# A gated MLP with a long convolution, forward and backward: regrouping the convolution's 64x32 passes on TensorE

## The chip, the cores and the metric

The kernel runs on one core of a Trainium2 chip. The metric is device time in microseconds, the median of several runs. The core's engines are called PE (TensorE, matrix products), DVE (VectorE), ACT (ScalarE), POOL (GpSimd) and SP (SyncE, which here only issues transfers). Each takes its own instructions in order, and they wait for each other by semaphores.

## The reference

It computes the sum of an input, a long-convolution branch (A) and a gated MLP (B), and the gradients of all weights and inputs from a given output gradient. Cut to what matters:

```python
def A(q, k, v, shift_k, ssm_k, ssm_D):          # S = 2048, D = 1024
    kv = shift4(k, shift_k) * v                  # four taps along time
    y = irfft(rfft(pad(kv)) * rfft(pad(ssm_k)))[:S]   # per channel, length 2 S
    return q * (y + kv * ssm_D)
def B(x, W_gate, W_up, W_down):                  # F = 3584
    gate = x @ W_gate
    return ((gate * (gate > 0)) * (x @ W_up)) @ W_down
xn = layernorm(A_q)
out = A_q + A(xn, k, v, shift_k, ssm_k, ssm_D) + B(xn, W_gate, W_up, W_down)
grads = vjp(out)(grad_out)                       # of all nine inputs but B_x
```

## The kernel before

**Two streams on one PE.** `LnMlp` yields the MLP's work step by step, eight 128x128 by 512 matmuls at a time, each step counted as some 1730 ns. `ABranch.steps` (line 587) yields the convolution as a list of slots. The loop at lines 1791 to 1802 counts nanoseconds and calls the next slot whenever the MLP's steps have paid for the last one: 1900 ns a slot while the MLP's forward part runs, and in the weight-gradient parts (`DENSE`, line 585) 1900 for a slot with products and 1250 for one without. So convolution products always stand between two MLP steps, and the order in each engine is written out by hand.

**The convolution.** The channels are done in eight groups of 128. Each length-4096 transform is factored into two small steps. In a group three spectra are needed: H (the filter), G (the incoming gradient times xn) and K (kv). Three products follow: GKV = H times conj(G), which gives the gradient of kv (`gkv`); K times conj(G), which gives the filter's gradient (`gh`); and K times H, which gives the output (`yt`). `cmul` (line 453) does half a product in five DVE steps; `turn` (446) prepares operands.

**Passes.** A slot may hold products. `fwd1`, `fwd1_filter`, `inv_a` and `inv_a_pair` use 32x64 tiles of PE (a "crossed" slot mixes an inverse step of this group with a forward step of the next). `f2`, `f2_pair` and `inv_b` use 64x32 tiles:

- `f2_pair(j, m)` (429) is the last forward step of G and K at once: two rounds of eight products of 256 columns.
- `f2(F, half, j)` (413) is the same for H alone: four rounds of eight products of 128 columns.
- `inv_b(st, key, half)` (512) is the last inverse step, two units, each one round of eight products of 512 columns.

Each such unit takes two of the eight PSUM banks (`banks`, 71); every bank is copied out by ACT (`act`, 85). A slot takes at most `cap` units: three, or two while the MLP's block of four simultaneous sums (`four`, line 1401) runs; what is over goes into a pass of its own (`parts`, 549). `tensor` (562) orders the rounds of a pass and puts the copies behind them.

**The arena.** One tile of nine parts of 8 KB per partition holds everything (line 132). Between the two small steps the data is turned by DVE transposes (`flip`, 338, two per call) into `flp`, which before is parts 0 and 1. G and K lie interleaved in parts 2 and 3, H in 4, `Cg`, `Ch`, `Cy` in 5 and 6, `Bg` and GKV in 7, `Bk` in 8. Part 0 is used for G before `f2_pair`, then for `gkv`, `yt` and `gh` before `inv_b`; part 1 for H before `f2` and for K before `f2_pair`.

**Loads and stores.** `fetch` (649) puts loads of the next groups into a list, from which one per slot is issued on SP, three slots later at the earliest, and not while `hold` is set (the last rows of an MLP block, or `cap` 2). `need` (272) issues what is still listed. `store` (105) issues on SP three slots later. `halo` (536) copies three rows between partitions.

**One group's passes before**, in order: three pair passes (3, 3 and 2 units), three 32x64 passes, `gkv`, `inv[1]`, crossed, crossed, `inv[2]`, two `f2` units, crossed, crossed, one `f2` unit with `yt`, one `f2` unit with `gh`. The `f2` units are the next group's H.

Of the kernel before, what the change touches and what calls it, by code (L numbers as in the profile page):

```python
# [17 lines left out]
P = 128  # L18
# [30 lines left out]
class ABranch:  # L49
# [27 lines left out]
    def evict(self, parts, view, out):  # L77
        for i, p in enumerate(parts):
            self.act(out(slice(i, i + 1)), p.rearrange(view))
# [49 lines left out]
    def open_arena(self):  # L129
        for _ in range(2):  # L130
            self.pools.pop().release()
        arena = self.pool("a_are", 1, side="right").tile([P, 9, NB1 * P], BF16, name="arena")
        self.flp = arena[:, 0:2, :].rearrange("p e (k c) -> p e k c", c=P)
        self.GK = arena[:, 2:4, :].rearrange("p s x -> p (s x)").rearrange("p (g b k i c) -> p g b k i c", b=2, k=2,
                                                                           i=2, c=P)
        self.G, self.K = self.GK[:, :, :, 0], self.GK[:, :, :, 1]
        spectrum = lambda i: arena[:, i, :].rearrange("p (g b i c) -> p g b i c", b=2, i=2, c=P)
        rows = lambda i: arena[:, i, :].rearrange("p (b cp u r i) -> p b cp u r i", cp=32, u=2, r=16, i=2)
        half = lambda i: arena[:, i, :].rearrange("p (bc q m i) -> p bc q m i", q=4, m=8, i=2)
        self.Bh = arena[:, 6, :].rearrange("p (b x cp n i) -> p b x cp n i", x=2, cp=16, n=NB1, i=2)  # L140
        self.Bg, self.Bk, self.H, self.GKV = rows(7), rows(8), spectrum(4), spectrum(7)
        self.Cg, self.Ch, self.Cy = half(5), half(5), half(6)
        self.Cs = arena[:, 5:7, :].rearrange("p s x -> p (s x)").rearrange("p (bc q m i) -> p bc q m i", q=4, m=8, i=2)

    def close(self):
# [283 lines left out]
    def f2_pair(self, j, m):  # L429

        def go():
            ps, at = self.banks("e b k i c", b=2, k=2, i=2)

            def part(ri):
                for q in range(4):
                    for e in range(2):
                        rows, l = slice(64 * e, 64 * e + 64), 8 * q + 2 * j + m
                        self.mm(at(e)[32 * q:32 * q + 32, :, :, ri, :], self.FW[rows, l, ri, :],
                                self.flp[rows, :, l, :].rearrange("p k (b c) -> p b k c", b=2))
            return [(256, lambda ri=ri: part(ri)) for ri in range(2)], lambda: self.evict(  # L440
                ps, "p e b k i c -> p (e b k i) c",
                lambda s: self.GK[:, 2 * j + s.start:2 * j + s.stop, :, :, :, 64 * m:64 * m + 64].rearrange(
                    "p e b k i c -> p (e b k i) c"))
        return go
# [117 lines left out]
    def tensor(self, p):  # L562

        if not isinstance(p, list):
            return self.run(p)
        units = [f() for f in p]
        first = [u for u in units if u[0][0][0] == 128][0:1]
        for rounds, _ in first if len({u[0][0][0] for u in units}) > 1 else []:
            rounds.pop(0)[1]()
        for rounds, _ in sorted(units, key=lambda u: -u[0][0][0]):  # L570
            for _, part in rounds:
                part()
        for _, evict in units:
            evict()

# [78 lines left out]
    def first(self, st):  # L654
        f1h, nx = self.fwd1_filter(st)[1], self.ahead(st, 1)
        yield f1h[0], lambda: self.gate_grad(st)
        yield None, None
        yield f1h[1], None
        self.load_k(st)
        f1g = self.fwd1(self.Bg, st["gt"])[1]  # L660
        yield None, lambda: self.add_D(st)
        flH = self.flip_H()
        yield f1g[0], flH
        yield None, flH
        yield f1g[1], None
        self.fetch(nx, self.load_g)
        f2H = [(1, self.f2(self.H, 1, j)) for j in range(4)]
        yield None, None
        flG = self.flip_B(self.Bg, 0)
        yield f2H[0:2], flG  # L670
        yield None, flG
        self.begin(st)
        tk = st["tk"]
        yield None, tk
        yield f2H[2:4], tk
        self.fetch(nx, self.load_xn)
        for _ in range(5):
            yield None, tk
        yield None, lambda: self.start_kvt(st)
        f1k = self.fwd1(self.Bk, st["kvt"])[1]  # L680
        yield None, None
        yield f1k[0], None
        yield None, None
        yield f1k[1], None
        self.fetch(nx, self.load_filter)
        yield None, None
        flK = self.flip_B(self.Bk, 1)
        yield None, flK
        yield None, flK
        yield None, None  # L690

    def slots(self, st, gi):
        G, K, H, GKV = self.G, self.K, self.H, self.GKV
        if gi == 0:
            yield from self.first(st)
        nx, n2 = self.ahead(st, 1), self.ahead(st, 2)
        last = nx is None
        f2 = [(1, self.f2_pair(j, m)) for j in range(4) for m in range(2)]
# [10 lines left out]
        yield None, None  # L709
        yield None, lambda: self.turn(G, 0, -1, slice(0, 4))  # L710
        q = self.cmul(H, G, True, GKV, 0)
        yield f2[6:8], q
        yield None, q
        yield None, q
        yield None, q
# [3 lines left out]
        q = self.cmul(H, G, True, GKV, 1)  # L719
# [13 lines left out]
        q = self.cmul(K, G, True, G, 0)  # L733
# [11 lines left out]
        yield None, q  # L745
        yield None, q
        q = self.cmul(H, K, False, K, 0)
        yield self.inv_b(st, "gkv", 0), q
        yield None, q
        yield None, q  # L750
        gkv = st["gkv"]
        gks = st["gks"] = self.ttile("gks")
        yield None, lambda: self.tt(gks[:, 0:16, :], gkv[:, 0:16, :], st["vt"][:], ALU.mult)
        self.fetch(nx, self.load_v)
        gv = self.ttile("gv")
        yield None, lambda: self.tt(gv[:, 0:16, :], gkv[:, 0:16, :], st["ksh"][:], ALU.mult)
        yield None, q
        self.store(self.gks_d[gi], gks[:, 0:16, :].rearrange("p r c -> p (r c)"))
        yield None, q
        self.store_time(self.out_gv, st["cg"], gv)  # L760
        yield [], lambda: self.halo(st)
        ia, inv = self.inv_a_pair()
        q = self.cmul(K, G, True, G, 1)
        yield None, q
        yield None, q
        yield inv[1], q
        yield None, q
        yield None, q
        q = self.cmul(H, K, False, K, 1)
        cross, gk = [inv[0], None], None  # L770
        if not last:
# [2 lines left out]
            self.fetch(n2, self.load_xn)  # L774
            cross = self.crossed(ia, self.fwd1(self.Bg, nx["gt"])[0], 0)
        yield None, q
        yield None, q
        yield cross[0], q
        yield None, q
        yield None, q  # L780
        f1g, cross = cross[1], [inv[3], None]
        f2H = []
        if last:
            yield None, None
            yield inv[2], None
        else:
            f2H = [(1, self.f2(H, 1, j)) for j in range(4)]
            self.need(self.load_k, nx)
            self.need(self.load_taps, nx)
            self.begin(nx)  # L790
            tk = nx["tk"]
            yield f1g, tk
            self.fetch(n2, self.load_g)
            yield None, tk
            yield None, tk
            yield inv[2], tk
            yield None, tk
            yield None, tk
            yield f2H[0:2], tk
            self.need(self.load_v, nx)  # L800
            yield None, lambda: self.start_kvt(nx)
            cross = self.crossed(ia, self.fwd1(self.Bk, nx["kvt"])[0], 3)
            yield None, None
# [11 lines left out]
        yield None, fly  # L815
        yield None, tg
        yield None, tg
        yield f2H[2:3] + self.inv_b(st, "yt", 0), None
        self.store_time(self.y_d, st["cg"], st["yt"])
        flh = self.flip_C(self.Ch, 0)  # L820
        yield None, flh
# [1 line left out]
        yield None, tg  # L823
        yield None, tg
        self.store_time(self.out_gk, st["cg"], gk)
        yield f2H[3:4] + self.inv_b(st, "gh", 0), None
        if last:
            yield None, None
            yield None, lambda: self.store_gh(st)
            return  # L830
        flG = self.flip_B(self.Bg, 0)
        yield None, flG
        yield None, self.both(lambda: self.store_gh(st), flG)
        flK = self.flip_B(self.Bk, 1)
        yield None, flK
        yield None, flK
        yield None, None
        yield None, None

# [3 lines left out]
class LnMlp:  # L843
# [271 lines left out]
    PACE = (2100, 1350)  # L1115

    def hidden(self, first, goT, load, ln, tables, Wg, Wu, Wd, g, xn_d, h_d, ug_d):


        nc, HS, N = self.nc, self.ST // 2, 2 * self.FB  # L1120
        w, sets, spare = first, (0, 1, 2), 3
        self.g_nat, self.hs = [None] * self.ST, [None] * (self.ST // 2)
        xT, gT = [], goT
# [713 lines left out]
```

## Time and profile before

| | |
|---|---|
| median of 3 runs | 1859.3 us (1858.87 to 1859.62) |
| profiled execution, its own time | 1858.79 us |
| its span | 1857.0 us |
| PE busy | 1850.1 us, 13061 matmuls |
| DVE busy | 1114.1 us |
| ACT busy | 645.7 us |
| SP's DMA queue q1 | 320.31 MB, 71.6% of 16 engines |
| clock granted to PE | 1.0 |
| convolution's first and last product (L83) | 125.0 and 1226.4 us |

The span is what the profile covers; the run's own time is 1.8 us longer. A line of the timeline has the start and length in microseconds, the engine, the kernel's line, the operation, what it writes and reads, the tile (rows*columns), the shape and how many instructions are merged; in brackets idle time before it and what ended it. A line of the waits has who waited, for whom, the microseconds in all, how often, and the longest.

### The profile page before, as it was taken

What the parts mean: (1) busy time and instruction counts of PE and PEld (TensorE: products, weight loads), DVE (VectorE), ACT (ScalarE), POOL (GpSimd) and SP (SyncE); (2) the same over time, 40 slices, a digit from 0 to 9 for tenths busy, and PEclk for the clock granted to TensorE, in tenths of its full rate; (3) what the DMA queues carried; (4) which work ended last, traced back from release to release, by engine and by line L of the source; (5) the groups of instructions that cost most, each with busy time, mean ns of one, the idle gap of its engine ahead of it and who ended that gap; (6) DMA issues with size and microseconds to landing.
All of it is one profiled execution on the core that took longest, in us unless ns stands there. A gap on an engine that the chain in (4) does not pass through costs nothing.

```text
span 1857.0 us, 32063 instructions
## 1 busy us (share of the span) xinstructions
PE 1850.1 (100%) x13061; PEld 845.7 (46%) x13061; DVE 1114.1 (60%) x1635; ACT 645.7 (35%) x1215; POOL 19.4 (1%) x51
## 2 busy tenths in 40 slices
PE   9999999999999999999999999999999999999999
PEld 4444444444444444444444444444444544444444
DVE  6656797797789767685694767621222222566652
ACT  5644444435444445545545454420000000111100
POOL 1000000000000000000000000000000000000000
PEclk9999999999999999999999999999999999999999
DMA  9897689967768766559566454379999857799973
GB/s 264 246 218 185 152 205 207 224 170 183 184 153 216 231 156 165 147 156 233 147 152 163 126 135 145 119 200 275 257 250 220 199 142 167 176 209 207 200 163 74
DMA packets 748132, 344.65 MB, mean 186 GB/s; under 512 B 576088, under 2 KB 715344, under 8 KB 747984
## 3 DMA queue, kind: packets, MB, share of 16 engines
q1 hardware_dynamic: 736848, 320.31, 71.6%
q10 hardware_dynamic: 9504, 17.04, 3.2%
q0 software_dynamic: 1632, 5.24, 0.8%
q8 instruction: 102, 1.67, 0.4%
q14 instruction: 46, 0.38, 0.1%
HBM read 143.79 MB, written 103.83 MB: 133 GB/s over the span
## 4 chain that ended last, share of the span: by engine, by line
PE 98%; SPq 1%; DMA 1%; DVE 0%; ACT 0%; issue 0%; ACTq 0%
PE ps_x L1689 21%; PE ps_w L1393 20%; PE ps_h L1058 10%; PE ps_o L1557 10%; PE ps_u L1058 10%; PE ps_g L1058 10%; PE ps_d L1393 9%; PE ps_c L83 4%; PE ps_d L1409 2%; PE ps_w L1409 1%; SPq L1076 1%; DMA goT<-in_grad_out_dram 0%; PE ps_r L1591 0%; DMA wg<-in_B_W_gate_dram 0%; DVE arena L344 0%
## 5 line engine op out<-in xcount | busy, mean ns | idle before, releaser
L1393 PE MATMUL ps_w<-ugs,xn_nat 128*128 128x512 bf16 x1728 | 381.3, 379 | 0.0
L87 ACT CAST arena<-ps_c 128x512 bf16<-128x512 f32 x576 | 294.0, 613 | 109.2 <-PE ps_c L83 109.0
L1058 PEld LDWEIGHTS <-xnT 128*128 128x128 bf16 x1792 | 172.0, 98 | 209.7 <-issue 5.7
L344 DVE STREAM_TRANSPOSE arena<-arena 128x1024 f32<-128x1024 f32 x96 | 179.5, 1931 | 133.1 <-ACT arena L87 117.0
L1393 PEld LDWEIGHTS <-xn_nat 128*128 128x128 bf16 x1728 | 165.2, 98 | 201.5 <-issue 7.3
L1058 PE MATMUL ps_u<-wu,xnT 128*128 128x512 bf16 x896 | 206.1, 379 | 0.1
L1058 PE MATMUL ps_g<-wg,xnT 128*128 128x512 bf16 x896 | 205.0, 379 | 0.6 <-DVE xnT L1102 0.3
L1058 PE MATMUL ps_h<-wdT,goT 128*128 128x512 bf16 x896 | 204.9, 379 | 0.6 <-DMA goT<-in_grad_out_dram 0.6
L1689 PE MATMUL ps_x<-wgT,ggT 128*128 128x512 bf16 x896 | 198.6, 379 | 0.0
L1689 PE MATMUL ps_x<-wuT,guT 128*128 128x512 bf16 x896 | 198.6, 379 | 0.0
L1707 ACT ACTIVATE w<-xn,m 128x512 f32<-128x512 bf16 x32 | 24.3, 807 | 480.2 <-DVE m L1700 366.8
L1557 PE MATMUL ps_o<-wd,hT 128*128 128x512 bf16 (+1 forms) x896 | 187.6, 372 | 0.0
L1393 PE MATMUL ps_d<-g_nat,hs 128*128 128x512 bf16 x768 | 170.1, 379 | 0.0
L1689 PEld LDWEIGHTS <-guT 128*128 128x128 bf16 x896 | 87.7, 98 | 105.7
L1689 PEld LDWEIGHTS <-ggT 128*128 128x128 bf16 x896 | 87.7, 98 | 105.5
L1058 PEld LDWEIGHTS <-goT 128*128 128x128 bf16 x896 | 85.7, 98 | 105.1 <-issue 2.9
L1557 PEld LDWEIGHTS <-hT 128*128 128x128 bf16 x896 | 87.7, 98 | 99.9
L1301 ACT CAST gh<-ps_h 128x512 bf16<-128x512 f32 x112 | 66.4, 594 | 184.4 <-PE ps_h L1058 175.0
L1396 ACT CAST wi<-ps_w 128x512 bf16<-128x512 f32 x108 | 64.6, 598 | 181.4 <-PE ps_w L1393 150.8
L1173 DVE SCALAR_TENSOR_TENSOR ru<-ru,ps_u 128x512 bf16<-128x512 bf16 x112 | 76.5, 683 | 71.9 <-PE ps_u L1058 49.3
L1549 DVE TENSOR_TENSOR ya<-ya,xe 128x1024 bf16<-128x1024 bf16 x16 | 11.1, 692 | 176.2 <-DMA xe<-xn_d 176.2
L91 DVE TENSOR_TENSOR t<-arena 128x2048 bf16<-128x2048 bf16 x96 | 113.9, 1219 | 0.4
(145 smaller groups left out, 1391.5 us busy)
## 6 DMA issues: line engine op xcount, KB each, us to landing
ugs<-ug_d SPq DMA_DIRECT2D x112, 256.0 KB
ug_d<-ru SPq DMA_DIRECT2D x110, 256.0 KB
wg<-in_B_W_gate_dram SPq DMA_DIRECT2D x56, 256.0 KB
wu<-in_B_W_up_dram SPq DMA_DIRECT2D x56, 256.0 KB
hs<-h_d SPq DMA_DIRECT2D x56, 256.0 KB
out_dram<-wi SPq DMA_DIRECT2D x56, 256.0 KB
h_d<-ht SPq DMA_DIRECT2D x108, 128.0 KB
gt<-in_grad_out_dram SPq DMA_DIRECT2D x32, 256.0 KB
```

What stands on the lines that cost most here:

```text
L83: self.pri.pin(self.nc.tensor.matmul(out, lhsT=lhsT, rhs=rhs, start=start, stop=stop))
L87: self.pri.pin(self.nc.scalar.copy(out=out, in_=in_))
L91: self.pri.pin(self.nc.vector.tensor_tensor(out=out, in0=in0, in1=in1, op=op))
L344: self.pri.pin(self.nc.vector.transpose(out=df[:, c0:c0 + 32, :], in_=sf[:, c0:c0 + 32, :]))
L1058: self.pri.pin(self.nc.tensor.matmul(ps[:], lhsT=xT[:, kt * P:(kt + 1) * P], rhs=w(kt), start=(kt == 0), stop=(kt == self.DT - 1)), always ...
L1173: return self.pri.pin(nc.vector.scalar_tensor_tensor(out=ru[s][:, 1, :], in0=ru[s][:, 0, :], scalar=0.0, in1=ps[:], op0=ALU.is_gt, op1=ALU ...
L1301: self.pri.pin(nc.scalar.copy(out=gh[:], in_=ps[:]))
L1393: self.pri.pin(self.nc.tensor.matmul(ps[:], lhsT=lhsT(st), rhs=rhs(st), start=(st == 0), stop=(st == self.ST - 1)))
L1396: self.pri.pin(self.nc.scalar.copy(out=out, in_=ps[:]))
L1409: self.pri.pin(self.nc.tensor.matmul(ps[i][:], lhsT=lhsT(i, st), rhs=rhs(i, st), start=(st == 0), stop=(st == self.ST - 1)))
L1557: nc.tensor.matmul(ps, lhsT=hT[:, kt, :], rhs=self.wd[:, kt, oc], start=(kt == 0), stop=(kt == self.FT - 1))
L1689: nc.tensor.matmul(ps, lhsT=T[:, kt, :], rhs=W[:, kt, oc], start=(i == 0), stop=(i == n - 1))
```

## The change

- `flp` becomes a view of all nine parts. G is turned into part 8 instead of part 0, after K has been turned out of part 8; `f2_pair` reads parts 1 and 8. G and K change places in their interleaved storage, and `Cy` and `Ch` change parts.
- Part 0 then stays free for `gh`, whose second half goes into the next group's third pair pass, with its stores. The first half shares a pass with the last two `f2` units.
- `gkv` comes six slots later, shares a pass with the first `f2` unit, and what hangs on it (gks, gv, their stores, the halo, the next `vt` load) moves with it; the K times H product moves ahead.
- The slot that held two `f2` units alone has no products any more. The crossed passes of G come one slot earlier.
- `tensor` orders a pass as one short round, the 512-column rounds, the other short rounds; with eight short rounds five come first.

The diff, cut:

```diff
-        self.flp = arena[:, 0:2, :].rearrange("p e (k c) -> p e k c", c=P)
+        self.flp = arena[:, 0:9, :].rearrange("p e (k c) -> p e k c", c=P)
...
-        self.G, self.K = self.GK[:, :, :, 0], self.GK[:, :, :, 1]
+        self.K, self.G = self.GK[:, :, :, 0], self.GK[:, :, :, 1]
...
-        self.Cg, self.Ch, self.Cy = half(5), half(5), half(6)
+        self.Cg, self.Cy, self.Ch = half(5), half(5), half(6)
...
-                                self.flp[rows, :, l, :].rearrange("p k (b c) -> p b k c", b=2))
+                                self.flp[rows, 1:9:7, l, :].rearrange("p k (b c) -> p b k c", b=2))
...
-        first = [u for u in units if u[0][0][0] == 128][0:1]
-        for rounds, _ in first if len({u[0][0][0] for u in units}) > 1 else []:
-            rounds.pop(0)[1]()
-        for rounds, _ in sorted(units, key=lambda u: -u[0][0][0]):
-            for _, part in rounds:
-                part()
+        short = [part for rounds, _ in units for n, part in rounds if n < 512]
+        at = 5 if len(short) == 8 else 1
+        for part in short[:at] + [part for rounds, _ in units for n, part in rounds if n == 512] + short[at:]:
+            part()
...
-        yield f2[6:8], q
+        if gi:
+            pv = self.sts[gi - 1]
+            yield f2[6:8] + self.inv_b(pv, "gh", 0)[1:], q
+            self.store_gh(pv)
+        else:
+            yield f2[6:8], q
...
         q = self.cmul(H, K, False, K, 0)
-        yield self.inv_b(st, "gkv", 0), q
+        for _ in range(5):
+            yield None, q
+        f2H = [] if last else [(1, self.f2(H, 1, j)) for j in range(4)]
+        ia, inv = self.inv_a_pair()
+        q = self.cmul(K, G, True, G, 1)
+        yield None, q
+        yield f2H[0:1] + self.inv_b(st, "gkv", 0), q
         yield None, q
         yield None, q
+        yield inv[1], q
         gkv = st["gkv"]
         gks = st["gks"] = self.ttile("gks")
         yield None, lambda: self.tt(gks[:, 0:16, :], gkv[:, 0:16, :], st["vt"][:], ALU.mult)
         self.fetch(nx, self.load_v)
+        self.store(self.gks_d[gi], gks[:, 0:16, :].rearrange("p r c -> p (r c)"))
         gv = self.ttile("gv")
         yield None, lambda: self.tt(gv[:, 0:16, :], gkv[:, 0:16, :], st["ksh"][:], ALU.mult)
-        yield None, q
-        self.store(self.gks_d[gi], gks[:, 0:16, :].rearrange("p r c -> p (r c)"))
-        yield None, q
         self.store_time(self.out_gv, st["cg"], gv)
-        yield [], lambda: self.halo(st)
...
-        yield None, q
+        yield [], lambda: self.halo(st)
         yield cross[0], q
         yield None, q
         yield None, q
-        f1g, cross = cross[1], [inv[3], None]
+        yield cross[1], q
+        self.fetch(n2, self.load_g)
+        cross = [inv[3], None]
...
-            yield f1g, tk
-            self.fetch(n2, self.load_g)
+            yield None, tk
...
-            yield f2H[0:2], tk
+            yield None, tk
...
-        yield f2H[2:3] + self.inv_b(st, "yt", 0), None
+        yield f2H[1:2] + self.inv_b(st, "yt", 0), None
...
-        yield f2H[3:4] + self.inv_b(st, "gh", 0), None
+        gh = self.inv_b(st, "gh", 0)
         if last:
+            yield gh, None
...
-        flG = self.flip_B(self.Bg, 0)
-        yield None, flG
-        yield None, self.both(lambda: self.store_gh(st), flG)
-        flK = self.flip_B(self.Bk, 1)
+        yield f2H[2:4] + gh[0:1], None
+        flK, flG = self.flip_B(self.Bk, 1), self.flip_B(self.Bg, 8)
         yield None, flK
         yield None, flK
+        yield None, flG
+        yield None, flG
```

The first group's own opening is changed in the same way: G is turned after K, into part 8.

## The prediction

> **What bounds the kernel now.** I read the page's busy shares, the chain that ended last and the table of waits first: they say whether time can be won anywhere but on TensorE.
>
> ```profile
> PE 1850.1 (100%) x13061; PEld 845.7 (46%) x13061; DVE 1114.1 (60%) x1635; ACT 645.7 (35%) x1215; POOL 19.4 (1%) x51
> PE 98%; SPq 1%; DMA 1%; DVE 0%; ACT 0%; issue 0%; ACTq 0%
> PE ps_warm L1113 <- POOL warm L1110: 1.5, 1, 1.5
> PE ps_c L83 <- ACT arena L87: 0.6, 1, 0.6
> ```
>
> PE is busy all the time, 98% of the chain is PE, and PE's longest waits are 1.5 and 0.6 us. So a change of the convolution's order is worth what it changes in PE's own stream, plus any wait that it adds. VectorE (60%) and ScalarE (35%) only have to be early enough.
>
> The second view is PE's timeline around single passes. A pass is one uninterrupted run of convolution products (L83) between matmuls of the MLP.
>
> ```profile
> 732.65 1.89 PE L1393 MATMUL ps_d<-g_nat,hs 128*128 128x512 bf16 x8
> 734.47 0.78 PE L83 MATMUL ps_c<-arena,FW 64*32 64x128 bf16 x64
> 735.18 3.63 PE L1393 MATMUL ps_d<-g_nat,hs 128*128 128x512 bf16 x16
> ...
> 750.78 3.19 PE L1393 MATMUL ps_d<-g_nat,hs 128*128 128x512 bf16 x14
> 753.90 0.25 PE L83 MATMUL ps_c<-arena,FW 64*32 64x128 bf16 x8
> 754.68 3.63 PE L1393 MATMUL ps_d<-g_nat,hs 128*128 128x512 bf16 x16
> ...
> 777.27 0.85 PE L83 MATMUL ps_c<-arena,FW 64*32 64x256 bf16 x48
> 778.05 5.35 PE L1393 MATMUL ps_d<-g_nat,hs 128*128 128x512 bf16 x24
> 783.34 0.63 PE L83 MATMUL ps_c<-arena,FW 64*32 64x256 bf16 x32
> 783.90 2.33 PE L1393 MATMUL ps_d<-g_nat,hs 128*128 128x512 bf16 x10
> ...
> 813.64 2.11 PE L1393 MATMUL ps_d<-g_nat,hs 128*128 128x512 bf16 x9
> 815.68 0.63 PE L83 MATMUL ps_c<-arena,RB 64*32 64x512 bf16 x16
> 816.24 2.12 PE L1393 MATMUL ps_d<-g_nat,hs 128*128 128x512 bf16 x9
> ```
>
> The reader is to take starts, not durations, because matmuls overlap. One MLP matmul takes 0.216 us from start to start (elsewhere 16 of them from 379.89 to 383.35). What a pass inserts is the start of the next MLP matmul minus the place where it would have stood. Two pair units (32 products of 256 columns): 783.90 - (778.05 + 24 x 0.216) = 0.67. Three pair units (48): 778.05 - 777.18 = 0.87, where 777.18 is 776.75 plus two steps. An inverse of two units (16 products of 512): 816.24 - 815.58 = 0.66. Two single forward units (64 products of 128): 735.18 - 734.38 = 0.80. One single forward unit with a whole inverse: 754.68 - 753.80 = 0.88. With the trace's finer digits these are 0.656, 0.874, 0.651, 0.802 and 0.874.
>
> Eight products of these tiles run side by side. From 0.656 to 0.874 two more eights of 256 columns were added, 0.11 each, so four cost 0.44 and **about 0.22 us of each pass is independent of what streams through it**. The 0.651 of the inverse gives the same (two eights of 512 at 0.21).
>
> **The change, part by part.** (1) *Passes.* The products are all kept; only their grouping changes. Per group of channels before: three pair passes (0.874, 0.874, 0.656), gkv alone 0.651, two forward units alone 0.802, forward unit + yt 0.874, forward unit + gh 0.874. After: pair, pair, pair + half of the earlier group's gh, forward + gkv, forward + yt, two forwards + half of gh. The first five have 0.874 each by streaming (0.22 + 0.64). The sixth has eight eights of 128 columns and one of 512: 0.22 + 0.43 + 0.21 = 0.87 plus an unknown e.
>
> Group 0 has no earlier gh and group 7 no forward units, so seven groups change 0.651 + 0.802 + 0.874 + 0.874 = 3.20 into 3 x 0.874 + e = 2.62 + e, and seven times the third pair pass grows by 0.218. The sum is 7 x (-0.58 + 0.22 + e), with the fine digits -2.53 + 7e, and 126 passes instead of 133.
>
> (2) *The unknown e.* No pass of before mixes 64 small products with eight long ones. The nearest rows bound it: the yt pass streams its 48 products with nothing on top (0 above), the pass of 64 small products costs 0.802 where streaming alone would give 0.65 (0.15 above). So e is 0 to 0.15. I take 0.03, near the yt row, since there too a long eight stands ahead of three short ones and gives the issuing time to catch up; only the first five shorts are exposed. The Trainium skill, "TensorE: Matmul & The Clock Gate", section "Architectural detail: the array is 16× 32×32, not 1× 128×128", gives PE a queue of 64 instructions, which 72 products with their weight loads overrun; by that alone e would be near 0.15 and the gain 0.7 us smaller. The yt pass has 96 instructions, overruns it too and pays nothing, so the row decides.
>
> (3) *Splits.* While the MLP's four-at-once blocks (L1401) hold four PSUM banks, a pass may have two units. Adding up the yields of both streams (which puts every pass of before where the trace has it) one of the merged passes falls there, group 2's last: 0.802 + 0.436 instead of 0.874 + e. Before, the same place cost 0.659 + 0.436 instead of 0.874. That is +0.14, and e counts six times. The pair of forward units at 858.38 stood in such a block and cost 0.08 more than its like; it is gone. So far: -2.53 + 0.14 - 0.08 + 6 x 0.03 = -2.29.
>
> (4) *Crossed passes one slot earlier.* In group 4 both crossed passes stand in such a block, and each needs six banks while the block holds up to four.
>
> ```profile
> 839.25 0.30 PE L83 MATMUL ps_c<-arena,IA 32*64 32x256 bf16 x4
> 840.35 0.89 PE L83 MATMUL ps_c<-gt,R 32*64 32x512 bf16 x4 [0.57 <-ACT arena L87]
> 841.17 1.04 PE L1409 MATMUL ps_d<-g_nat,hs 128*128 128x512 bf16 x4
> ```
>
> This first one inserted 2.01 where its like inserts 0.66: 1.35 us for a bank. It stays where it is. The second (846.67) cost nothing; it moves eight matmuls earlier, when one more bank still waits for a copy of some 0.6 us. Bounds 0 and 1.35; I take 0.4.
>
> (5) *Moved VectorE work.* gks, gv, the input's product and both flips change order, 96 transposes and all multiplications stay. In the dense part VectorE has finished the last input of the next pass well ahead: the last flip before a pair pass ends some 3 us ahead, and after the change three of those distances shrink by eight matmuls (1.7 us) to about 1.2 us. Cost 0; with that cover gone, up to 1 us each. (6) *SP and POOL.* gh's stores go some eleven slots later and gks/gv's stores stand ahead of the halo loads, same number; the next vt load is asked for seven slots later. POOL's memset stays in its place. Cost 0, except in the third rival. (7) *The strided read* of parts 1 and 8 in one operand: same columns, another distance; no row shows one, and 0 to the smallest difference between passes (0.02) bounds it, so 0.
>
> Sum: -2.29 + 0.4 = -1.9 us of the profiled execution's 1858.79 (span 1857.0 and 1.8 around it), 1856.9; that execution lies 0.5 under the median, so **1857.4**.
>
> **The rivals.** *ScalarE's copies set the pace.* Fuller passes need six banks at once.
>
> ```profile
> 338.94 3.04 ACT L87 CAST arena<-ps_c 128x512 bf16<-128x512 f32 x6
> 344.64 0.58 ACT L1301 CAST gh<-ps_h 128x512 bf16<-128x512 f32 x1 [2.66 <-DMA h_d<-ht]
> ```
>
> Six copies take 3.04 us; the closest passes are 16 matmuls and one pass apart, 4.3 us, which leaves room for two other copies. But ScalarE takes its work in order: here one copy waited 2.66 us for a store, and the pass at 344.41 inserted 1.46 instead of 0.87. New is that the copy of the first forward unit overwrites H while VectorE's product may still read it. In group 4 that product's fourth step ends about 17.9 us after the pass at 802.80 (its steps taken from 805.63 on), the copy is due at 19.1; 88 matmuls apart instead of 80, the others have 2.8. If VectorE is over 1.2 to 2.8 us later there, ScalarE stands, and each of seven groups pays one such stall, 0.59 to 1.35, say 1.0: 1857.4 + 7 = **1864.4, slower**. The Trainium skill, "TensorEngine Tiling (Array Packing)", section "PSUM Bottleneck", says that tiling quickens TensorE but not the emptying of PSUM, which can become the limit; by it this rival is the likelier one. Against it stand the pairs of six-unit passes of before at the same distance (772.93 and 777.27), without a wait. 5%.
>
> *Issue, not the switch, is the price.* If small products cost 9 ns each (0.58 / 64) wherever they stand, e is 0.15 and the crossed pass pays 0.8: 1859.3 - 2.47 + 0.9 + 0.8 = **1858.5**. 14%.
>
> *A late load.* In group 4 the load of vt for group 5 now becomes due inside a four-at-once block, is held back, and is forced out one slot before its use. A vt load takes 5.3 us from first issue (820.58) to its last small packets (about 826), the product 1.22. Issued behind the eight ugs loads (857.9) it would hold up the next crossed pass by 2 to 3 us: **1859.9**; ahead of them (851.8), as program order has it, nothing. 8%.
>
> *Stalls go as well*: gh's stores leave the crowded place at 344, and the 0.59 and most of 1.35 vanish: **1855.7**. 7%. *It doesn't do what it says*: most merged passes are split by the bank limit and the 0.22 us stay: **1859.3**. 2%.
>
> **How the numbers follow.** The forecast holds 64%: 1857.4. Range 1855.8 to 1860.5: from a little above "stalls go" over both bounds of e and of the crossed pass to the late load. A measurement of this kernel tells about 0.2% (3.7 us) from no change. Faster by more (under 1855.6): the lower half of "stalls go", 4%. Slower by more (over 1863.0): the first rival and a few stalls of other origin, 6%. Within: 90%.
>
> **What would show it.** Right: 126 passes; seven of 0.87 each for pair + gh, forward + gkv; the sixth at 0.87 to 0.92; no new row in PE's waits but some tenths at the second crossed pass near 843. Wrong: the sixth at 1.0 (e), PE rows waiting for "ACT arena" in several groups, or PE waiting for "DVE kp" in group 4.

## The result and the profile after

The changed kernel takes 1866.02 us (median of 6 runs, 1863.39 to 1868.04); the kernel before took 1859.13 (6 runs, 1858.81 to 1859.62) in the same comparison. The ratio is 1.0037 with a 95% interval of [1.0024, 1.005]: slower by 0.37%, where 1857.4 was forecast and 1860.5 was the upper end. The profiled execution took 1868.04 us, its span 1866.3 against 1857.0 before, so 9.3 us have to be found.

The busy line of the page after, some of PE's waits, and PE's and ACT's timelines where the longest wait stands:

```profile
PE 1837.0 (98%) x12845; PEld 848.0 (45%) x13061; DVE 1115.0 (60%) x1635; ACT 645.7 (35%) x1215; POOL 19.4 (1%) x51
```
```profile
PE ps_g L1058 <- ACT gh L1301: 5.6, 1, 5.6
PE ps_w L1393 <- issue: 3.0, 19, 0.2
...
PE ps_c L83 <- DVE kp L91: 0.9, 1, 0.9
PE ps_h L1058 <- DVE ru L1173: 0.7, 1, 0.7
PE ps_c L83 <- DVE arena L344: 0.7, 1, 0.7
```
```profile
340.80 0.85 PE L83 MATMUL ps_c<-arena,FW 64*32 64x256 bf16 x48
341.58 1.90 PE L1058 MATMUL ps_g<-wg,xnT 128*128 128x512 bf16 x7
349.13 3.57 PE L1058 MATMUL ps_g<-wg,xnT 128*128 128x512 bf16 x8 [5.65 <-ACT gh L1301]
```
```profile
339.18 0.58 ACT L1301 CAST gh<-ps_h 128x512 bf16<-128x512 f32 x1 [4.58 <-PE ps_h L1058]
348.49 0.58 ACT L1301 CAST gh<-ps_h 128x512 bf16<-128x512 f32 x1 [8.73 <-DMA h_d<-ht]
348.97 3.04 ACT L87 CAST arena<-ps_c 128x512 bf16<-128x512 f32 x6
```

DVE and ACT do the same work as before, to 0.9 us and to the digit. PE's busy time is no measure here: 216 of 13061 matmul records are missing, and the "issue" row (19 waits of at most 0.2 us) is holes in the record, not time. The weight loads are complete, so all inserted times below go by their starts, as the forecast's went by matmul starts. By this measure a pass of three units inserts 0.883 in the trace of before as well.

The other rows are new. The first is the news: group 1's first pair pass (340.80) has six full banks, and its copies stand on ACT behind the copy of an MLP bank (`gh` of line 1301, not the filter's gradient of the same name) that waits 8.73 us for a store of `ht`, the MLP's hidden block, to land. `ht` and this `gh` take turns in the same five buffers (`e1_tile`), so the copy has nowhere to write until the store has read its buffer. Until 348.49 no bank is emptied, and the MLP runs out of banks after one more sum.

Over what the passes and the MLP would take by their own classes, this execution loses: **8.64 us near 349**, 1.35 at the first crossed pass near 848 (as before), 1.15 at a crossed pass near 871 (waits for `kp`, which waits for vt), 0.80 near 248 (`ru`, the MLP's pair tile, into which DVE empties a bank), 0.78 near 181 (`arena`, a transpose), 0.33 near 323 (`wu`, a load that SP brings late), 0.29 near 329 (`ru` again), 0.51 at the second crossed pass near 854, 0.41 near 642 (a bank that waits for the copies of a six-bank pass), 0.10 near 388. The sixth passes lose 0.68 together. Before had its own: 1.35 near 839, 0.57 near 344, 0.39 near 484. The sum: -2.47 (passes) + 0.68 + 0.51 + 0.78 + 0.80 + 8.64 + 1.15 + 0.62 + 0.41 + 0.10 - 0.57 - 0.39 = +10.3; the first 38 us, which the change doesn't touch, were 1.0 shorter in this execution. That gives 9.3.

### The profile page after: what moved, and what is told of

The parts are those of the page before. It is cut to its first block, busy times and chain, and to the rows that moved or that the text cites. A ratio compares the mean times of both kernels' runs of the same rounds, so it can differ in the third digit from the quotient of the medians.

```text
span 1866.3 us, 31860 instructions
## 1 busy us (share of the span) xinstructions
PE 1837.0 (98%) x12845; PEld 848.0 (45%) x13061; DVE 1115.0 (60%) x1635; ACT 645.7 (35%) x1215; POOL 19.4 (1%) x51
## 4 chain that ended last, share of the span: by engine, by line
PE 94%; DVE 2%; DMA 1%; issue 1%; ACT 0%; SPq 0%; POOL 0%; DVEq 0%; ACTq 0%; POOLq 0%
PE ps_x L1689 21%; PE ps_w L1393 20%; PE ps_o L1557 10%; PE ps_u L1058 10%; PE ps_g L1058 10%; PE ps_h L1058 9%; PE ps_d L1393 9%; PE ps_c L83 4%; PE ps_d L1409 1%; DVE arena L344 1%; DMA vt<-in_A_v_dram 0%; DVE ru L1173 0%; DMA wu<-in_B_W_up_dram 0%; PE ps_r L1591 0%; DMA h_d<-ht 0%
## 5 line engine op out<-in xcount | busy, mean ns | idle before, releaser
L1393 PE MATMUL ps_w<-ugs,xn_nat 128*128 128x512 bf16 x1676 | 374.9, 379 | 4.8 <-issue 3.0
```

The source lines that it names most:

```text
L1393: self.pri.pin(self.nc.tensor.matmul(ps[:], lhsT=lhsT(st), rhs=rhs(st), start=(st == 0), stop=(st == self.ST - 1)))
```

## The experiments

The theory: **the copies of one pair pass stand behind a copy that waits for a late store**. It has two halves, the place of the pass and the lateness of SP. The rival: the loss is the price of fuller passes (the first rival of the forecast), and stands in many places. Each comparison has its own runs of the kernel before on the same chip: 1858.60 us for the first four kernels, 1858.79 for the next four, then 1858.32, 1858.63 and 1858.48.

### Place and stores: four kernels

**shift_after** is the changed kernel with one empty slot less at the end of group 0, **shift_before** the kernel before with one more.

```diff
-        yield None, None
+        if gi:
+            yield None, None
```

> The changed kernel with one empty slot less at the end of group 0, so that group 1's first pair pass stands after 1432 MLP matmuls, as before the change, and not after 1440. Theory 'place': the long wait near 341 us is there because this pass came to stand behind the ScalarE copy that waits for a store; back at its old place the loss there falls from 8.6 to about 0.6 us and the kernel takes 1858 to 1860 us. Rival 'fuller passes': the pass holds six banks wherever it stands and the merged passes are what costs; the time stays at 1863 to 1868 us.

> The kernel of before with one more empty slot at the end of group 0, so that its pair pass stands after 1440 matmuls, where the change puts it; nothing merged. Theory 'place': the wait of several us and perhaps the lower clock appear here too, 1862 to 1867 us. Rival 'fuller passes': 1859 to 1860 us, as before.

Measured: shift_after 1860.18 us, ratio 1.0015 [1.0006, 1.0024]; shift_before 1861.94, ratio 1.0016 [1.0006, 1.0026]. Each against its own runs of the kernel before, one slot takes the changed kernel's excess from 6.9 to 1.6 us, and adds 3.3 to the kernel before. The trace of shift_before then shows the same picture, smaller (it is the fastest of its ten executions, 1859.67; the slowest took 1864.02):

```profile
343.39 0.59 ACT L1303 CAST gh<-ps_h 128x512 bf16<-128x512 f32 x1 [4.85 <-DMA h_d<-ht]
343.87 3.04 ACT L87 CAST arena<-ps_c 128x512 bf16<-128x512 f32 x6
```

So the place is one half: before, the pass came between two `gh` copies, and its banks were emptied while the second waited. It is not the whole. In the trace of shift_after the second copy waits longer than before,

```profile
346.49 0.59 ACT L1302 CAST gh<-ps_h 128x512 bf16<-128x512 f32 x1 [3.56 <-DMA h_d<-ht]
```

the next pair pass loses 1.48 us where the kernel before loses 0.57, and two of its ten executions took 1865.14 and 1866.05 us, at a mean clock of 0.998.

**pool_after** and **pool_before** put the stores of `ht` from MLP blocks 6 and 7 on GpSimd's queue.

```diff
-                        queue = nc.gpsimd if n == 0 and s < 4 else nc.sync
+                        queue = nc.gpsimd if n == 0 and s < 4 or n in (6, 7) else nc.sync
```

> The changed kernel with the stores of ht in the MLP's blocks 6 and 7 issued by GpSimd instead of SP, so that they do not stand behind SP's transposes and the convolution's transfers. Theory 'store': ScalarE's copy no longer waits 8.7 us, the loss near 341 us goes and the kernel takes 1858 to 1860 us. Rival 'fuller passes' or 'banks': the copies are too slow by themselves, the time stays at 1863 to 1868 us.

> The kernel of before with the same stores on GpSimd, as control. Theory 'store': the 0.6 us that before loses at 344 us goes, 1858.5 to 1859.2 us. Rival: GpSimd's issuing costs something of its own, 1859.3 us or more, and then the same amount is to be taken off the run with the changed kernel.

Measured: pool_after 1859.63 us, ratio 1.0006 [0.9997, 1.0016]; pool_before 1857.66, ratio 0.9996 [0.9987, 1.0006]. ACT of pool_after, with the pass in the same place:

```profile
341.21 0.59 ACT L1301 CAST gh<-ps_h 128x512 bf16<-128x512 f32 x1 [1.14 <-PE ps_h L1058]
341.69 3.04 ACT L87 CAST arena<-ps_c 128x512 bf16<-128x512 f32 x6
```

The copy waits for its product only, and the whole 8.64 are gone. Against the kernel before in the same comparison the excess falls from 6.9 to 1.0 us, so 5.9 us of the changed kernel's time hang on these stores, and 0.9 of that of before. What is left of the change, 1859.63 - 1857.66 = +2.0 instead of -1.9, is in the small waits; the next kernels go into them.

### The small waits, one by one

All three are pool_after with one more edit. **v_pool**: vt's load is not held back by the four-at-once blocks.

```diff
-    a.hold = lambda: b.hold or a.cap == 2
+    a.hold = lambda: b.hold or a.cap == 2 and a.queue[0][0] != a.load_v
```

> The stores of the MLP's blocks 6 and 7 are on GpSimd's queue, as in the kernel that gave 1859.63 us, and a load of vt is no longer held back while the MLP's four-at-once blocks run. If the late load of vt is what one crossed pass waits for (1.01 us near 862.7 in the profile of that kernel, 1.15 near 871 in the changed one), that loss goes and the time falls by about 1.0, to 1858.6. If the load would have been late anyway, or the pass waits for VectorE for another reason, the loss stays and the time is 1859.6.

Measured 1858.91 us. The loss near 862 is gone from the trace. The third rival thus happened, at its place, but in a form that it had excluded: in the trace of after the load is issued at 861.92, straight ahead of the eight ugs loads (864.09), and the product still gets vt only at 870.99, 9.1 us after the issue where the forecast had taken 5.3.

**gkv_pool**: the pass of one `f2` unit and `gkv` one slot later.

```diff
-        yield f2H[0:1] + self.inv_b(st, "gkv", 0), q
         yield None, q
+        yield f2H[0:1] + self.inv_b(st, "gkv", 0), q
```

> Stores on GpSimd's queue as before; the merged pass of one forward unit and the inverse for gkv stands one slot (eight MLP matmuls) later in every group. If the 0.78 us near 248 are a place (six banks asked for just when VectorE is a product behind with the MLP's own bank), the loss there goes or moves and the time falls by up to 0.8, to 1858.9. If the sixfold pass pays this wherever it stands beside VectorE's products, a loss of 0.5 to 0.8 stays within 4 us of the pass and the time is 1859.6.

Measured 1858.32 us; no loss is left near 248. The timeline of pool_after shows what it was:

```profile
249.13 0.68 DVE L1173 SCALAR_TENSOR_TENSOR ru<-ru,ps_u 128x512 bf16<-128x512 bf16 x1
...
249.87 1.89 PE L1058 MATMUL ps_h<-wdT,goT 128*128 128x512 bf16 x7 [0.72 <-DVE ru L1173]
```

The merged pass takes six banks where `gkv` alone took four, and the MLP's next bank is one that DVE empties (`ru`) only at 249.13, behind a product's last step (two sums, 1.29 us from 247.93). This is a fuller pass's price at this place, 0.78 us large. Two more waits for a bank stand behind merged passes: in the trace of pool_after PE waits for `ru` a second time, 0.31 us behind group 0's last pass (0.47 by weight loads, near 328), and at 633 a sum of the four-at-once block waits 0.2 us for the copies of a six-bank pass (0.41 by weight loads). The first of these is gone in first_pool, the second stays even in best2_b. The trace of gkv_pool also has 0.59 instead of 1.01 at the late load.

**first_pool**: an empty slot taken from the end of group 0 and put ahead of its first pair pass.

```diff
         yield None, flG
         yield None, flG
         yield None, None
+        yield None, None
```

> Stores on GpSimd's queue as before; one empty slot is taken from the end of group 0 and put ahead of its first pair pass, so that from group 1 on every pass stands where the change has it. If the 0.77 us near 181 are the second transpose of a pair (G's now the last, since it lies where K's input was), which ends after the pass is due, that loss goes and the time falls by about 0.77, to 1858.9. The passes inside group 0 move by a slot, so the loss near 248 may change as well, between 0 and 0.8: 1858.1 to 1858.9. If the pass waits for something else, 1859.6.

Measured 1858.21 us, the 0.77 near 181 gone, and the 0.78 near 248 with it; 0.36 appear at 340 and 0.56 near 278, where best1's trace names a late load of the MLP's weights (wu, 0.35).

**best1** joins the four edits, **best2** puts the second crossed pass back behind the product's last step (the slot it had before), **best2_b** is best2 again, beside **pool_before_b**.

> All four edits together: stores on GpSimd's queue, vt's load not held back, the merged gkv pass a slot later, the empty slot ahead of the first pair pass. If the losses are separate and each goes, 1859.63 - 1.0 - 0.8 - 0.8 = 1857.0, a little under the kernel before with the same stores on GpSimd's queue (1857.66), and about 2 under the kernel before: the fewer passes would then be worth what the forecast said. If each removed wait comes back at the next place, 1859 or more.

> The four edits that gave 1857.61 us (stores on GpSimd's queue, vt's load not held back, gkv's pass a slot later, an empty slot ahead of the first pair pass), and the second crossed pass of the transition back to the slot after the first product's last step, eight MLP matmuls later, as it was before the change. If step 4 of the forecast is right in its mechanism (a bank that still waits for a copy), the 0.51 us near 845 go and the time is 1857.1. If the loss is the four-at-once block itself, it stays at 0.4 to 0.5, 1857.6; the next inverse pass is now eight matmuls closer, and its copies could give up to 0.5 back.

```diff
-        yield cross[1], q
+        late = cross[1]
+        yield None, q
         self.fetch(n2, self.load_g)
...
-            yield None, tk
+            yield late, tk
```

Measured: best1 1857.61 us, ratio 0.9996 [0.9987, 1.0004]; best2 1856.82, ratio 0.9994 [0.9985, 1.0003]. The 0.51 at the second crossed pass are gone from best2's trace, so step 4 was right in mechanism (a bank that waits for a copy) and nearly in size.

> The kernel before with the stores of the MLP's blocks 6 and 7 on GpSimd's queue (1857.66 in the earlier comparison), again, beside the next kernel on the same chip: 0.5 to 1.0 under the kernel before.

> The changed kernel with five edits (stores on GpSimd's queue, vt's load not held back, gkv's pass a slot later, an empty slot ahead of the first pair pass, the second crossed pass back in its slot; 1856.82 earlier). If the change is worth what its passes save once its waits are gone, this is 1.0 to 2.0 under the kernel before and 0.3 to 1.2 under the kernel before with the same stores on GpSimd's queue. If the whole gain came from the stores, the two are equal within 0.3.

Measured on one chip: pool_before_b 1857.76 us, ratio 0.9996 [0.9987, 1.0005]; best2_b 1856.78, ratio 0.9992 [0.9984, 1.0001]. The change with its waits taken away is 1.0 below its counterpart. That is the expected side of the two, and all passes together insert 97.67 us in best2_b and 99.13 in pool_before. But both intervals reach 1, and the two overlap, so it is an indication. best2_b is the fastest version seen, 1.9 under the kernel before.

**at_pool**: in the sixth pass the eight long products stand after the first short one.

```diff
-        at = 5 if len(short) == 8 else 1
+        at = 1
```

> Stores on GpSimd's queue; in the passes of two forward units and half an inverse the eight long products stand after the first short one, not after five. Read from the trace: these passes now insert 0.963 (four of them) and 1.14 (two). If the long products give the issuing time to catch up, an earlier place gives 0.90 to 0.96, the time falls by 0 to 0.3; if every small product costs its issuing time wherever it stands, 0.96 stays; if the long eight then wait for their operand or their banks, 1.0 or more.

Read from one trace: four of these passes insert 1.026 us instead of 0.963, the other two 1.14 as in pool_after (in after and best2_b the first of these two has 0.97). The place of the long products matters, by 0.06; so it is not a fixed price of each small product ("issue, not the switch"), but earlier is worse, not better. What costs the 1.14 stays open.

### Why SP was late

**after_again** and **before_again** are the two kernels unchanged.

> The changed kernel once more, unchanged, for a second trace. If the copies of group 1's first pair pass stand behind a copy that waits for a store, PE's longest wait is again a gate product of the MLP near 349 behind that copy, of 4 to 7 us, and the time is 1863 to 1868, longer where the granted clock shows less than 1.0. If the wait of the first trace was an accident of that execution, it stands elsewhere or is under 1 us, and the time is about 1860.

> The kernel before, once more, for a second trace. In its first trace the four transposes of the next activations took SP 5.95 us from 316.61 on; in the changed kernel they took 8.76 and 7.40 us, and all of SP's later issues were as much later. If the longer issuing comes with the changed order, this trace shows 5.9 to 6.1 again and the gh copy near 344 waits 2.5 to 2.8 us for its store. If it varies from one execution to the next whatever the order, it may show 7 to 8.8, the gh copy then waits up to 5 us, and the pass near 344 loses more than 0.57, up to 2; the time is still 1858 to 1860.

Measured: after_again 1864.33 us, ratio 1.0031 [1.0019, 1.0043], the same wait at the same place, 3.5 us long; before_again 1858.07. SP's issues of the two first traces, before and then after (start, length, what, how many):

```profile
245.87 1.40 SPq L99 DMA_DIRECT2D vt<-in_A_v_dram  x2
...
281.98 2.97 SPq L1082 DMA_TRANSPOSE xnT<-xn_d  x2
...
304.67 1.97 SPq L1051 DMA_DIRECT2D wg<-in_B_W_gate_dram  x4
...
316.61 5.95 SPq L1082 DMA_TRANSPOSE xnT<-xn_d  x4
...
341.36 1.17 SPq L1184 DMA_DIRECT2D h_d<-ht  x1
```
```profile
277.10 2.34 SPq L99 DMA_DIRECT2D vt<-in_A_v_dram  x2
...
289.43 2.69 SPq L1082 DMA_TRANSPOSE xnT<-xn_d  x2
...
310.08 2.03 SPq L1051 DMA_DIRECT2D wg<-in_B_W_gate_dram  x4
...
317.23 8.76 SPq L1082 DMA_TRANSPOSE xnT<-xn_d  x4
...
345.24 2.09 SPq L1184 DMA_DIRECT2D h_d<-ht  x2
```

The reader is to compare row by row: SP is 7.45 us later at the first transposes, 5.4 at wg, 0.6 at the next transposes, and then 3.9 at the store, mostly because those transposes take 8.76 us instead of 5.95. In the second traces they take 7.40 (after_again) and 6.33 (before_again), and wg is issued at 310.74 and 303.82: the lateness at wg goes with the changed order, and its last part varies from execution to execution. From 307 to 314 the first trace of before has some 6 us in which SP issues nothing, after has 1.

What was moved: group 0's halo copies, the stores of gks and gv, and vt's load, 2.1 + 0.4 + 1.4 + 2.3, some 6.3 us of issuing, from the stretch 246 to 258, where SP had time, to 261 to 279.

**v_late_before** is the kernel before with vt alone asked for seven slots later (the `fetch` line moved behind `inv[1]`); **v_free** the changed kernel with vt alone held back by nothing.

```diff
-    a.hold = lambda: b.hold or a.cap == 2
+    a.hold = lambda: (b.hold or a.cap == 2) and a.queue[0][0] != a.load_v
```

> The kernel before with one edit: vt is asked for seven slots later in every group, as in the changed kernel. If this is what makes SP late, the load comes out near 277 here too, the transposes that start at 281.98 start 3 to 7 us later, the store that the gh copy near 344 waits for comes 1 to 4 us later, and the pass near 344 loses 1.5 to 4 us instead of 0.57; the late load of group 5 may cost up to 1.2 more: 1860 to 1863. If the move of vt is harmless by itself, 1858.6.

> The changed kernel, stores on SP's queue, with one edit: the loads of vt are held back by nothing, neither by the blocks of four rows nor by the four-at-once blocks. In the changed kernel group 0 asks for vt seven slots later, its load falls into a block that holds loads back and comes out at 277.10 instead of 245.87, where SP has no free time; from there on SP is 5 to 7 us later than before, and the store that a copy waits for near 349 comes 2 to 4 us later. If that move is what makes SP late, vt's load now stands near 260, the transposes that start at 289.4 start 2 to 5 us earlier, PE's wait near 349 falls from 3.5 to 5.7 us to 0 to 2.5, and the late load near 871 (1.15) goes too: 1859 to 1862. If SP is late for the halo's and the gradients' stores that moved as well, SP is as late as before and only the 1.15 go: 1863 to 1865.

Measured: v_late_before 1858.99 us, ratio 1.0004 [0.9995, 1.0013]; v_free 1865.19, ratio 1.0039 [1.0026, 1.0053]. One of SP's lines of v_late_before, then two of v_free:

```profile
284.24 4.21 SPq L1082 DMA_TRANSPOSE xnT<-xn_d  x2
```
```profile
262.12 2.32 SPq L99 DMA_DIRECT2D vt<-in_A_v_dram  x2
...
275.20 1.98 SPq L1051 DMA_DIRECT2D wu<-in_B_W_up_dram  x4
```

vt's move alone makes SP 2.2 us late (281.98 to 284.24, 304.67 to 306.86), which the free time after it nearly swallows: the store is issued at 341.63, 0.3 later than before, and the pass there loses 1.09 instead of 0.57. So vt alone does not carry the loss; of the two expectations the first, 1860 to 1863, was wrong. In v_free vt comes out at 262, still inside the full stretch: the first transposes are issued at 289.43 as in after, SP issues wu at 275.20 instead of 270.86, PE waits for it twice (1.89 and 0.83), and the wait for the `gh` copy is still 2.8. The sum of the moves, 6.3 us, is near the 7.45 that SP is late at 289, but that is no account of it: transfers that did not move also take SP longer to issue there (the `sD` load 3.38 us in after, 1.80 in before, 1.96 in v_free). That the halo's and the gradient stores' share makes the rest is argued from the order; it was not tried alone.

### Two that leave the stores on SP

**e1_after** is the changed kernel with six buffers for `ht` and `gh`, and five instead of six for the MLP's pair tile `ru` to make room.

```diff
-        self.e2 = tc.alloc_tile_pool(name="b_e2", bufs=6, side="left")
-        self.e1 = tc.alloc_tile_pool(name="b_e1", bufs=5, side="left")
+        self.e2 = tc.alloc_tile_pool(name="b_e2", bufs=5, side="left")
+        self.e1 = tc.alloc_tile_pool(name="b_e1", bufs=6, side="left")
```

> The changed kernel with its stores where they were, on SP's queue, and six buffers instead of five for the tile that the store of the hidden block is read from and the gradient copy is written to; to make room, the buffers of the MLP's pair tile are five instead of six. If the copy waits for the landing of a store five tiles back, it now waits for an older one, some 1.7 to 2 us earlier: the 5.65 us wait of PE near 349 falls by about 2 us, the stretch at half clock with it, and the time is 1860 to 1864. If SP's late start delays everything alike, the wait stays at 5 to 6 us. The fewer pair tiles may cost up to some us elsewhere, where a store of a pair tile lands late; that shows as other waits, in the MLP's four-at-once blocks above all.

Measured 1866.24 us, ratio 1.0042 [1.0028, 1.0056]. ACT's lines:

```profile
341.07 0.58 ACT L1301 CAST gh<-ps_h 128x512 bf16<-128x512 f32 x1 [1.14 <-PE ps_h L1058]
...
351.64 0.60 ACT L1166 ACTIVATE ru<-ps_g 128x512 bf16<-128x512 f32 x1 [6.54 <-DMA ug_d<-ru]
```

The `gh` copy at 341.07 no longer waits, although SP issues the store that it waited for in after only at 342.33 (345.24 in after, 341.36 in before): the buffer was the tie. Then the tile that lost a buffer takes its place. ACT waits 6.54 us for a store of `ru`, and the next pair pass stands behind that. PE waits 4.41 us for it. The expected 1860 to 1864 failed; only who waits has changed.

**best_sp** is best2 with all stores on SP and, instead of the slot ahead of the first pair pass, shift_after's slot less.

> The changed kernel with all stores on SP's queue, and instead of the empty slot ahead of the first pair pass one slot less at the end of group 0, which puts group 1's first pair pass where it stood before the change (1860.18 alone); vt's load not held back, gkv's pass a slot later, the second crossed pass back. If the place of that pass is all that the stores cost, this gives 1860.18 - 0.8 - 0.5 = 1858.9, less up to 1.0 where the late load also occurred. If SP's late stores cost something at every place near it, 1860 to 1861, with single executions of 1862 to 1866.

Measured 1859.96 us (1857.8 to 1864.46), ratio 1.0011 [1.0002, 1.002]. In its trace SP's transposes take 8.75 us, the `gh` copy waits 4.53, and the pass behind it, now the second, loses 2.35. Place alone does not save the change while SP is late.

## Why the prediction was wrong, step by step

*What bounds the kernel* was right, and so was the reading that a wait is what can spoil it.

*Step 1, passes*: right. 126 passes; the median of those with three units is 0.883 by weight loads, as before. With the stores off SP and the waits taken away, the gain shows (best2_b).

*Step 2, e*: mis-sized. Four passes have 0.08, one 0.09, one 0.26, together 0.68 where 0.18 stood. *Step 3, splits*: as forecast.

*Step 4*: 0.51 for a forecast of 0.4, with the mechanism named.

*Step 5, moved VectorE work at 0*: failed at two places, within its own price ("up to 1 us each"): 0.78 at group 0's first pair pass, where G's transpose is now the last, and 0.80 at gkv's. The distances were counted in groups of the dense part; group 0 has its own opening (`first`), which I did not count.

*Step 6, "SP and POOL moves, cost 0"*: this step failed, and with it the forecast. The wait behind SP, which this step put at 0, cost 8.64 us in the first trace, and by the medians 5.9 us go when those stores leave SP. I checked what is moved and for whom it comes late, but not what it is moved into. Around 260 to 300 SP issues with hardly a pause, and with 6.3 us of issuing put there SP is late, some 65 to 85 us later, at a store that an ACT copy waits for. The store and the copy are shown by the experiments; how the lateness splits among the moved transfers is open, but for vt's 2.2 us. The place of the copies, the other half, stood in no step of the sum: shift_before, where SP's transfers keep their old order, loses 3.3 us by it.

*Step 7, the strided read at 0*: right, the pair passes that read parts 1 and 8 insert what they did before.

*The first rival* had the right mechanism (ACT takes its work in order, and all copies stand behind one that waits) with the wrong trigger and price: not H's copy in seven groups at 1.0 each, but one MLP copy, 8.64 us. The line that I quoted for it, `gh` waiting 2.66 us at 344.64, was the place. The same adding up of yields that served step 3 puts group 1's first pair pass one MLP step later; laid beside that line it says that the pass's copies come behind the waiting copy instead of ahead of it. *The late load* did happen (1.15), *stalls go as well* did not.

## What to carry to other kernels

- When an order written by hand shifts by one step, look in the trace of before for the copies that already wait for a store, and ask on which side of them each moved copy falls. A wait of 2.66 us that cost PE 0.57 became one of 8.73 that cost it 8.64; the place alone cost 3.3.
- Price a moved DMA by the queue it lands in: list SP's free time over the next 50 us. The 6 us free between 307 and 314 are what kept v_late_before on time: 2.2 us late at 306.86, 0.3 at the store.
- A buffer that a store must free is only as early as that store. One more buffer moved the wait to the tile that gave it up.

## What the runs showed of the hardware

**A stall costs more than its length.** The granted clock of the changed kernel, two-microsecond windows (the columns are the length, the busy time of PE, weight loads, DVE, ACT and POOL, then clock, DMA share and GB/s):

```profile
350.00:352.00 2.00, 2.00 (x6) 0.67 (x5) 0.00 (x0) 2.00 (x6) 0.00 (x0) 0.50 0.88 182
...
354.00:356.00 2.00, 2.00 (x45) 0.89 (x50) 0.33 (x1) 0.02 (x1) 0.00 (x0) 0.77 1.12 357
```

The clock is 0.5 for 6.83 us at the 5.65 us wait, from 1.1 us ahead of its end on, for 3.41 at waits of 3.5 (after_again) and 4.4 (e1_after), and stays at 1.0 after waits of 1.8 (shift_before) and 2.8 (v_free near 351). So the wait was 5.65 of the 8.64 us, and the rest, 2.99, is close to half of the 5.8 us in which PE works at that clock. The Trainium skill, "TensorE: Matmul & The Clock Gate", section "Part 1: The HAM clock gate", gives half rate after an idle window of about 3.4 us, and 3413 ns for a window; the stretches of 3.41 and twice that agree. The same page, section "Why this matters for your kernels", advises against PE gaps of over about 3 us. The trace shows that to be not enough: v_free near 280 had half clock for 3.41 us at the end of two waits of only 1.89 and 0.83, with four products between them.

**A transpose's issue can stand.** While the convolution runs, SP needs 1.3 to 1.7 us to issue most of the DMA transposes (nine in ten of the 59 in the trace of before; the later ones take up to 9.6). The second of the four near 319 took 4.28 in the first trace of after (1.54 before), while the traffic fell to a fifth of the 216 GB/s that before has there:

```profile
318.00:320.00 2.00, 2.00 (x11) 0.94 (x10) 0.28 (x1) 2.00 (x5) 0.00 (x0) 1.00 1.79 326
320.00:322.00 2.00, 2.00 (x11) 0.89 (x10) 1.57 (x2) 0.92 (x2) 0.00 (x0) 1.00 1.30 41
```

With the stores on SP, the four take 5.9 to 6.5 us where wg's loads were issued 9 to 12 us ahead of them (before, before_again, shift_before, v_late_before), 7.1 to 8.8 where it was 6.5 to 7.2 (after, after_again, shift_after, e1_after, best_sp), and 7.85 at 9.5 (v_free), where wu came late as well. The distance is not the whole of it: in pool_before and pool_before_b, with the order of before and those stores on GpSimd's queue, they take 7.6 and 8.3 us at 9.4. What the transpose waits for in those microseconds no trace here shows.
